# Chunked attention and gated convolution on one core: all pieces in a new order, buffers in new homes, nine first taps on VectorE

## The chip, the cores and the metric

One core of a Trainium2 chip. The core has five instruction queues: TensorE (PE in the rows, with its weight loads as PEld), VectorE (DVE), ScalarE (ACT), GpSimd (POOL) and SyncE (SP), which issues all transfers here. Each works through its own queue in order and waits on semaphores for the others. The metric is the time of one execution on the device in microseconds, lower is better.

## The reference

```python
# q, k, v: (8 batches, 8 heads, 576 tokens, 64); chunks of 64 tokens
scores = scale * np.matmul(q_c, k_c.transpose(0, 1, 2, 4, 3))   # 64 x 64 in each chunk
scores = scores - np.max(scores, axis=-1, keepdims=True)
attn = np.exp(scores)
attn = attn / (np.sum(attn, axis=-1, keepdims=True) + 1e-09)
out = np.matmul(attn, v_c)
x = np.ascontiguousarray(attn_out.transpose(0, 2, 1, 3)).reshape(B, S, H * D)   # (8, 576, 512)
for k in range(K):                                  # 5 taps along the tokens, per channel
    gate_pre += conv_w[k][None, None, :] * xp[:, k:k + S, :]
gate = 1.0 / (1.0 + np.exp(-gate_pre))
val = x @ w_val                                     # 512 x 512
return (gate * val @ w_out).astype(np.float32)      # 512 x 512
```

## The kernel before

The 8 x 576 tokens are cut into nine groups of 512 tokens. The kernel is written as short functions, called **pieces**, each one or a few instructions on one engine. A string, `ORDER`, lists some 1,130 pieces with their arguments; the loop at L599 calls them one after the other, and since `run` (L157) keeps the program order, that list is the order of every engine's queue. A second table, `SLOTS`, gives the number of the buffer that each new tile takes, in the order in which tiles are made; a tile that takes a used buffer waits until its last reader is done. So the two tables decide all waits. The time per piece, the planner that made the tables, and its model are not in the program.

For a group `g` and a half `p` of its heads, the pieces are, with their engine:

- `lq`, `lk`, `lv`: load q, k, v (SyncE, 512 KB each); `lw v c`, `lw o c`: load a quarter of the two weight matrices (512 KB); `lc`: the taps.
- `S g p b`: scores (PE, 64 x 64 tiles, into one of two PSUM buffers `big`); `mx`: row maximum (VectorE); then either `sb` (subtract, VectorE), `ex` (exp, ScalarE), `sm` (sum and reciprocal, VectorE), or `ng` (VectorE) and `ea` (sixteen exps with sums, ScalarE) and `rc` (VectorE).
- `nm`: multiply by the reciprocal (GpSimd; `nmD` on VectorE); `T`: transpose (PE into `big`); `ec`: copy out of PSUM (ScalarE; `ecD` on VectorE); `A`: attention times v (PE into `big`).
- `xc g p u`: one half of x out of PSUM (ScalarE; `xcD` VectorE); `xr`: x rounded (ScalarE); `xd`: the rest, x minus the rounded x (VectorE, reads PSUM). Instructions of two engines that touch one PSUM buffer are kept apart, reads too: `xc` placed behind an `xd` of the same buffer waits for it.
- `k0 g h`: first tap of the convolution for a quarter `h` of the channels (ScalarE; `k0D` VectorE, `k0G` GpSimd); `k g h j`: the other four taps (VectorE, 144 pieces); `sg`: tanh, which is the gate (ScalarE).
- `V g m c`: x times `w_val`, three matmuls per piece (rounded and rest of both factors), into one of four PSUM banks `ps`; `vc`: copy out (ScalarE) and `gs`: gate times value (VectorE), or `gm`, both in one straight out of PSUM (VectorE).
- `gr`: round (ScalarE); `gd`: the rest (GpSimd; `gdD` VectorE); `P g t c`: times `w_out`, three matmuls per piece, into `ps`; `oc`: copy out (ScalarE; `ocD` VectorE); `st`: store (SyncE).
- `w1` to `w7`, `wb`, `w9`: make rounded and rest parts of the weights (`w1`, `w3` and `w7` on VectorE or, with a G, GpSimd; `w4` VectorE; `w2`, `w5`, `w6` ScalarE; `wb` GpSimd, `wbD` VectorE). `F`: the first group's product with unprepared weights (PE). `W n`: n matmuls of zeros that keep PE busy. `hl`, `zr`, `zi`, `zm`, `zw`: small fills.

PE has 3,333 matmuls in all. All instructions carry the line of `run`, L158, in the rows, so tiles and shapes tell them apart: `acc` is the convolution's accumulator, `x` the attention's output, `ps` and `big` PSUM, `t`, `t2a` and the like working buffers of a pool, `v_hi`, `v_lo`, `o_hi`, `o_lo` the weights.

Of the kernel before, what the change touches and what calls it, by code (L numbers as in the profile page):

```python
# [17 lines left out]
ORDER = """zi,lk 0 0,zw,zr 1,lc,lq 0 0,lw v 2,lk 0 1,w1 c 0,S 0 0 1,w3G c 0,lq 0 1,lw v 0,mx 0 0 1,sb 0 0 1,S 0 0 0,lw v 3,  # L18
lk 1 0,W 4,ex 0 0 1,S 0 1 0,mx 0 0 0,lv 0 0,zr 0,zm,sb 0 0 0,sm 0 0 1,w5 c 0,S 0 1 1,w3G v 2,W 8,hl 0,w1G v 2,
ex 0 0 0,lq 1 0,nm 0 0 1,sm 0 0 0,T 0 0 1,w5 v 0,w2 c 0,lw v 1,w2 v 2,mx 0 1,w3 v 0,w1 v 0,lk 1 1,nm 0 0 0,w5 v 2,  # L20
mh 0 1,ec 0 0 1,T 0 0 0,ml 0 1,w4 v 2,ec 0 0 0,sp 0 1,w2 v 0,A 0 0 0,w4 c 0,ep 0 1,xc 0 0 0,lw o 0,w1 v 3,lq 1 1,
w3G v 3,lv 0 1,w7G v 2,w4 v 0,w9,A 0 0 1,w5 v 3,w5 v 1,w7 v 0,lk 2 0,S 1 0 0,w1G v 1,S 1 0 1,sm 0 1,w3 v 1,mx 1 0,
F 0 1 0,nm 0 1,lw o 3,F 0 2 0,k0 0 0,w6 v 0,xc 0 0 1,w2 v 3,sb 1 0,w2 v 1,w1G o 0,F 0 3 0,T 0 1,w4 v 3,S 1 1 0,w6 v 2,
lq 2 0,ec 0 1,S 1 1 1,ex 1 0,wb v 2,w4 v 1,wb v 0,A 0 1,lw o 2,lk 2 1,w7 v 3,w5 o 0,W 8,F 0 0 0,w7G v 1,lv 1 0,k0 0 1,
xr 0 1,F 0 2 1,mx 1 1,sm 1 0,w3G o 0,lq 2 1,sb 1 1,k 0 0 4,w1 o 3,S 2 0 0,xc 0 1 0,w2 o 0,nm 1 0,k 0 0 2,ex 1 1,
sm 1 1,xc 0 1 1,w6 v 3,S 2 0 1,xn 0 1,xe 0 1,F 0 3 1,V 0 2 2,hl 1,mx 2 0,T 1 0,sb 2 0,w6 v 1,w3 o 3,w5 o 3,w4 o 0,
F 0 1 1,nm 1 1,k 0 0 1,lq 3 0,S 2 1 0,S 2 1 1,lk 3 0,ec 1 0,lw o 1,ex 2 0,k0 0 3,A 1 0,lv 3 0,F 0 0 1,w5 o 2,mx 2 1,
w7G o 0,xc 1 0 1,wb v 3,sm 2 0,w5 o 1,sb 2 1,w1G o 2,V 0 3 2,lv 1 1,V 0 1 2,k 0 0 3,V 0 0 2,k0G 0 2,w1G o 1,xr 1 0,
w3G o 1,V 0 2 3,w6 o 0,k 0 1 1,T 1 1,xd 1 0,w2 o 2,nm 2 0,xc 1 0 0,ex 2 1,lq 4 0,V 0 0 3,V 0 3 3,ec 1 1,w2 o 3,vc 0 3,
S 3 0 0,wbD v 1,A 1 1,S 3 0 1,k 0 2 4,vc 0 2,k0 1 0,V 1 1 0,V 1 2 0,xr 1 1,sm 2 1,V 1 2 1,mx 3 0,lk 3 1,xd 1 1,  # L30
V 1 1 1,xc 1 1 0,lq 3 1,lv 3 1,ng 3 0,k 0 2 1,V 0 1 3,V 1 2 2,xc 1 1 1,sg 0 0,T 2 0,w3 o 2,lv 2 0,k 0 1 2,V 1 1 2,
gm 0 0,V 1 3 0,k 0 1 4,k 0 3 2,k 0 2 3,nm 2 1,w4 o 3,ea 3 0,k 0 3 1,V 1 2 3,k 0 1 3,k0 1 3,V 1 3 1,V 1 1 3,T 2 1,
V 1 3 2,k 0 3 4,ec 2 0,k 0 2 2,ec 2 1,S 3 1 0,k 0 3 3,vc 1 1,k0G 1 2,S 3 1 1,A 2 0,V 1 0 0,gr 0 0,w2 o 1,V 1 0 1,
rc 3 0,lk 4 0,mx 3 1,vc 1 2,k 1 0 2,hl 2,xr 2 0,V 1 0 2,sb 3 1,gd 0 0,sg 0 2,nm 3 0,xc 2 0 1,V 1 3 3,sg 0 1,W 1,
vc 1 3,xc 2 0 0,xd 2 0,k 1 2 1,gs 0 2,gm 0 1,V 1 0 3,ex 3 1,lv 2 1,w4 o 2,sm 3 1,S 4 0 0,S 4 0 1,A 2 1,vc 1 0,k0G 1 1,
k 1 0 3,V 2 0 0,xc 2 1 0,xc 2 1 1,lk 4 1,mx 4 0,k0 2 1,xr 2 1,w7 o 2,k0G 2 0,ng 4 0,k 1 0 4,V 2 1 0,sg 0 3,V 2 1 1,
wb o 0,nm 3 1,gr 0 2,V 2 0 1,k 1 1 4,lq 4 1,V 2 2 0,xn 2 1,xe 2 1,V 2 3 0,V 2 2 1,V 2 3 1,k 1 2 4,ea 4 0,T 3 0,w4 o 1,
V 2 1 2,V 2 0 2,ec 3 0,V 2 2 2,V 2 1 3,V 2 2 3,k 1 1 3,V 2 3 2,k 1 3 3,lq 5 1,vc 2 1,T 3 1,k 1 1 2,k 1 3 1,vc 2 2,
k 1 1 1,V 2 3 3,S 4 1 0,ec 3 1,vc 2 3,k 1 2 2,S 4 1 1,gr 0 1,A 3 0,k 1 3 2,k 1 0 1,sg 1 0,k 1 3 4,V 2 0 3,xr 3 0,
k 1 2 3,vc 2 0,w7 o 1,lv 4 0,gd 0 1,xc 3 0 1,P 0 2 0,w6 o 1,P 0 3 0,P 0 1 0,gd 0 2,P 0 0 0,xcD 3 0 0,xd 3 0,gs 0 3,  # L40
w6 o 2,gr 0 3,wbD o 1,A 3 1,hl 3,w7 o 3,P 0 1 1,P 0 2 1,P 0 0 1,sg 1 2,mx 4 1,ng 4 1,wbD o 2,xr 3 1,gd 0 3,k 2 0 2,
k 2 1 4,P 0 3 1,w6 o 3,wbD o 3,rc 4 0,ea 4 1,P 0 3 2,P 0 1 2,k 2 0 1,xd 3 1,xcD 3 1 1,gs 1 0,P 0 2 2,P 0 0 2,P 0 0 3,
oc 0 0,k0G 2 2,k 2 0 3,P 0 1 3,P 0 3 3,nm 4 0,lq 5 0,oc 0 1,P 0 2 3,k0 2 3,sg 1 1,T 4 0,k 2 1 2,k 2 0 4,V 3 3 0,
xc 3 1 0,k 2 2 2,oc 0 2,V 3 1 0,lk 5 0,rc 4 1,V 3 0 0,gs 1 2,lk 5 1,k 2 3 2,V 3 1 1,ec 4 0,sg 1 3,gs 1 1,S 5 0 0,
sg 2 0,S 5 1 0,k0 3 3,k 2 1 1,S 5 0 1,oc 0 3,S 5 1 1,gs 1 3,mx 5 1,gr 1 0,gd 1 0,nm 4 1,V 3 1 2,gr 1 2,V 3 1 3,
k 2 1 3,V 3 3 1,V 3 2 0,lq 6 0,mx 5 0,V 3 0 1,lk 8 0,k0 3 0,gr 1 1,k 2 2 3,sb 5 0,vc 3 1,sg 2 1,V 3 3 2,ng 5 1,
gdD 1 2,V 3 3 3,lv 4 1,gr 1 3,k 2 2 4,k0 3 2,k 2 3 1,V 3 2 1,gd 1 1,V 3 0 2,lk 6 0,vc 3 3,k 2 3 3,P 1 0 0,ea 5 1,
P 1 1 0,P 1 1 1,k 2 2 1,k 3 2 4,k 3 3 1,lq 6 1,gdD 1 3,P 1 1 2,k 2 3 4,V 3 2 2,k 3 0 2,T 4 1,V 3 0 3,k 3 2 3,k 3 0 1,
# [610 lines left out]
```

## Time and profile before

| | |
|---|---|
| median of 3 runs | 283.56 us (281.74 to 283.76) |
| the profiled execution | 281.89 us |
| its span, first to last instruction | 280.1 us |
| mean granted TensorE clock | 0.994 |
| PE busy | 258.9 us (92%) |
| VectorE busy | 239.3 us (85%) |
| ScalarE busy | 195.2 us (70%) |
| GpSimd busy | 113.1 us (40%) |
| HBM read, written | 32.53 MB, 9.44 MB |

Busy times are unions of an engine's instructions; a PE that is busy may still run its matmuls slowly. The 1.79 us between span and execution lie around the program.

### The profile page before, as it was taken

Reading aid. Unit: us, or ns where it says so; the run is one execution under the profiler, and the core shown is the slowest. Engines: PE = TensorE matmul, PEld = TensorE weight load, DVE = VectorE, ACT = ScalarE, POOL = GpSimd, SP = SyncE. Lnnn points to the kernel's source line nnn. Section 1 sums busy time; section 2 is a strip of 40 time slices with the busy share of each in tenths; the row PEclk is TensorE's granted clock in tenths of the full one; section 3 lists DMA queues with packets and bytes.
Section 4 is the critical chain, followed back from the end, with each engine's and each line's share of the span. In section 5 each row is a group of like instructions: output and inputs, shape, how many; then the busy total and the mean of one; then the engine's idle time right before and its main releaser. Section 6 shows DMA issues by size and latency. Waiting matters only on the chain.

```text
span 280.1 us, 7958 instructions
## 1 busy us (share of the span) xinstructions
PE 258.9 (92%) x3333; PEld 216.6 (77%) x3333; DVE 239.3 (85%) x330; ACT 195.2 (70%) x499; POOL 113.1 (40%) x92
## 2 busy tenths in 40 slices
...
PEclk9999999999999999999997999999999999999999
...
GB/s 230 414 412 411 400 280 53 216 92 288 77 64 239 3 94 210 150 136 170 75 118 0 307 145 192 0 120 220 6 37 0 111 5 152 0 171 16 115 187 150
DMA packets 14291, 42.47 MB, mean 152 GB/s; under 512 B 1712, under 2 KB 1712, under 8 KB 14256
## 3 DMA queue, kind: packets, MB, share of 16 engines
...
q8 instruction: 26, 0.43, 0.7%
q14 instruction: 9, 0.07, 0.1%
HBM read 32.53 MB, written 9.44 MB: 150 GB/s over the span
## 4 chain that ended last, share of the span: by engine, by line
DVE 53%; PE 21%; ACT 14%; DMA 5%; issue 5%; SPq 0%; DVEq 0%; ACTq 0%
DVE acc L158 22%; PE ps L158 19%; DVE t L158 9%; DVE mx L158 5%; DVE rs L158 5%; ACT t L158 5%; DVE e_row L158 4%; ACT e_row L158 4%; DMA acc<-in_moe_w_val 4%; ACT x L158 2%; PE big L158 2%; DMA ld<-in_q 2%; DVE t2q L158 1%; DVE x L158 1%; DVE t4a L158 1%
## 5 line engine op out<-in xcount | busy, mean ns | idle before, releaser
L158 DVE SCALAR_TENSOR_TENSOR acc<-x,cw,acc 128x516 f32<-128x516 f32 (+1 forms) x144 | 111.7, 817 | 3.2 <-ACT acc L158 2.9
L158 PE MATMUL ps<-t,v_hi 128*128 128x512 f32 x240 | 85.1, 395 | 2.9 <-ACT t2f L158 2.1
L158 PEld LDWEIGHTS ps<-t,v_hi 128*128 128x128 f32 x240 | 45.5, 190 | 11.5 <-ACT t2f L158 2.5
L158 PE MATMUL ps<-t,v_lo 128*128 128x512 f32 x120 | 45.9, 383 | 0.0
L158 POOL TENSOR_TENSOR t<-e_row,rs 128x1024 f32<-128x1024 f32 (+1 forms) x12 | 23.2, 1936 | 30.0 <-DVE rs L158 30.0
L158 PEld LDWEIGHTS big<-ld,ld 64*64 64x64 f32 x1152 | 19.5, 139 | 15.0 <-issue 9.7
L158 ACT ACTIVATE e_row<-big,mx 128x64 f32<-128x64 f32 x96 | 28.6, 357 | 2.5 <-DVE mx L158 2.5
L158 PE MATMUL big<-ld,ld 64*64 64x64 f32 x1152 | 22.0, 226 | 8.7 <-DMA ld<-in_q 6.6
L158 PE MATMUL ps<-o_hi,t 128*128 128x512 f32 x80 | 29.9, 381 | 0.0
L158 ACT COPY x<-big 128x512 f32<-128x512 f32 (+3 forms) x42 | 19.7, 520 | 12.5 <-PE big L158 6.2
L158 DVE TENSOR_REDUCE mx<-big 128x16 f32<-128x1024 f32 (+1 forms) x19 | 21.8, 1151 | 5.1 <-PE big L158 5.1
L158 PEld LDWEIGHTS ps<-t,v_lo 128*128 128x128 f32 x120 | 22.8, 190 | 3.3 <-issue 0.5
L158 ACT ACTIVATION_READ_ACCUMULATOR e_row<-big,mx 128x1 f32 x96 | 23.8, 249 | 0.0
L158 PE MATMUL big<-t,ld 64*64 64x64 f32 x1088 | 19.4, 220 | 4.4 <-issue 2.4
L158 PEld LDWEIGHTS big<-t,ld 64*64 64x64 f32 x1088 | 17.6, 135 | 6.7 <-issue 2.1
L158 ACT COPY t<-ps 128x512 f32<-128x512 f32 x27 | 16.7, 625 | 8.4 <-PE ps L158 5.8
L158 ACT ACTIVATE t<-big 128x1024 f32<-128x1024 f32 x15 | 15.8, 1077 | 7.1 <-PE big L158 7.1
L158 ACT ACTIVATE e_row<-e_row 128x1024 f32<-128x1024 f32 (+1 forms) x12 | 12.0, 1001 | 11.4 <-DVE e_row L158 11.4
L158 ACT CAST t<-big 128x1024 fp32r<-128x1024 f32 x17 | 17.3, 1019 | 2.0 <-PE big L158 2.0
L158 ACT ACTIVATE acc<-x,cw 128x516 f32<-128x516 f32 (+1 forms) x24 | 17.8, 756 | 0.0
L158 POOL TENSOR_SCALAR acc<-x,cw 128x516 f32<-128x516 f32 (+1 forms) x9 | 14.9, 1657 | 4.8 <-ACT x L158 4.8
L158 PEld LDWEIGHTS ps<-o_hi,t 128*128 128x128 f32 x80 | 15.1, 189 | 2.2
...
## 6 DMA issues: line engine op xcount, KB each, us to landing
...
```

The lines of the kernel that those rows point to most:

```text
L158: return tc.keep_in_program_order(fn(*args, **kwargs))
```

## The change

The two tables are new; no function changes. Counted by piece, first taps go from 24 on ScalarE, 3 on VectorE and 9 on GpSimd to 16, 9 and 11; the rest `gd` from 25 on GpSimd and 11 on VectorE to 18 and 18; output copies `oc` from 28 on ScalarE and 8 on VectorE to 31 and 5; `gm` from 2 to 3 (and `vc` and `gs` from 34 to 33); `xcD` from 4 to 5; one `w1` goes from VectorE to GpSimd, and one `wb` from VectorE to GpSimd. All other pieces keep their engine and number, PE's matmuls, the loads and the 21 matmuls of zeros among them. The order of loads at the start is new, and the homes of all buffers are dealt out anew.

```diff
-ORDER = """zi,lk 0 0,zw,zr 1,lc,lq 0 0,lw v 2,lk 0 1,w1 c 0,S 0 0 1,w3G c 0,lq 0 1,lw v 0,mx 0 0 1,sb 0 0 1,S 0 0 0,lw v 3,
...
+ORDER = """lq 0 0,zw,lk 0 0,lw v 0,zr 0,S 0 0 0,S 0 0 1,mx 0 0 0,zr 1,sb 0 0 0,mx 0 0 1,W 8,w1 v 0,lc,sb 0 0 1,ex 0 0 1,lw v 3,
...
-    ld="012345012350412305241203123142135013450420534024035425",
...
+    ld="012345012345012345012345123152130512341520412513202401",
...
```

VectorE's queue around `xd 2 0`, the subtraction that releases PE's `A 2 1`. Before (`t44` with `big0` is `xd 2 0`, `acc` are taps, `t2q` is `w4 o 2`, preparing a weight):

```order
L158 TENSOR_REDUCE mx1_990<-big1_906 128x16
L158 SCALAR_TENSOR_TENSOR acc1_785<-x1_541,cw_70,acc1_785 128x516
L158 TENSOR_TENSOR e_row1_65<-big1_906,mx1_990 128x16x64
L158 TENSOR_TENSOR t44_1022<-big0_943,t47_998 128x1024
L158 SCALAR_TENSOR_TENSOR acc3_880<-x1_541,cw_70,acc3_880 128x516
L158 SCALAR_TENSOR_TENSOR t2a_1025<-t22_1006,t2o_783 128x512
L158 SCALAR_TENSOR_TENSOR t28_1027<-t26_1014,ps0_347 128x512
L158 SCALAR_TENSOR_TENSOR t2q_838<-t2k_659,t2q_838 128x512
```

and after (`t4b` with `big0` is `xd 2 0`, the ISA row is `w7 o 3`, `t2i` is `w4 o 2`, `acc2<-x1` the first tap of group 1 that has come from ScalarE):

```order
L158 ISA t2f_475<-t2f_475,t2h_493 128x1024
L158 SCALAR_TENSOR_TENSOR acc0_521<-x0_151,cw_70,acc0_521 128x512
L158 SCALAR_TENSOR_TENSOR acc1_347<-x0_151,cw_70,acc1_347 128x512
L158 SCALAR_TENSOR_TENSOR acc0_521<-x0_151,cw_70,acc0_521 128x512
L158 SCALAR_TENSOR_TENSOR acc1_347<-x0_151,cw_70,acc1_347 128x512
L158 SCALAR_TENSOR_TENSOR acc0_521<-x0_151,cw_70,acc0_521 128x512 x2
L158 SCALAR_TENSOR_TENSOR t2i_654<-t2l_665,t2i_654 128x512
L158 TENSOR_REDUCE mx1_989<-big1_909 128x16
L158 TENSOR_TENSOR e_row1_65<-big1_909,mx1_989 128x16x64
L158 TENSOR_SCALAR acc2_906<-x1_668,cw_70 128x516
L158 TENSOR_TENSOR t4b_1064<-big0_943,t48_1009 128x1024
```

Two weight pieces of `w_out` and a first tap now stand ahead of the subtraction.

ScalarE's queue behind `xr 5 0`. Before (`t42` is `xr 5 0`, `x1<-big1` are the copies `xc 5 0 0` and `xc 5 0 1`, `t2n` the tanh `sg 3 3`, `t44` is `xr 5 1`, `t2f` is `oc 2 3`, the copy that empties the bank for `V 5 1 0`):

```order
L158 CAST t42_2196<-big1_2140 128x1024
L158 COPY x1_2129<-big1_2140 128x2x256
L158 ACTIVATE t2n_2214<-acc1_1571 128x192
L158 ACTIVATE t2n_2214<-acc1_1571 128x320
L158 CAST t44_2220<-big0_2094 128x1024
L158 COPY t2f_2230<-ps0_1996 128x512
L158 COPY t2i_2236<-ps1_2067 128x512
L158 COPY x1_2129<-big1_2140 128x2x64
L158 COPY x1_2129<-big1_2140 128x2x192
```

and after (`x1<-big1` 64 and 192 wide is `xc 5 0 1`, `t2k` is `vc 4 2`, `t49` is `ec 6 0`, `t2o` is `oc 2 3`, `t2q` is `oc 2 0`, the last row is `xc 5 0 0`):

```order
L158 COPY x1_2149<-big1_2082 128x2x64
L158 COPY x1_2149<-big1_2082 128x2x192
L158 COPY t2k_2237<-ps0_1980 128x512
L158 ACTIVATE t49_2240<-big0_2217 128x1024
L158 COPY t2o_2248<-ps2_2151 128x512
L158 COPY t2q_2255<-ps3_2069 128x512
L158 ACTIVATE t2e_2257<-acc2_1533 128x192
L158 ACTIVATE t2e_2257<-acc2_1533 128x320
L158 COPY x1_2149<-big1_2082 128x2x256
```

The half of the x copy that has `xd 5 0` ahead of it has moved behind the copies out of `ps`.

VectorE's queue near its end. Before, the last piece that a matmul's bank hangs on is `gs 8 1` (`t2q`), with these pieces around it:

```order
L158 SCALAR_TENSOR_TENSOR acc2_3336<-x0_3265,cw_70,acc2_3336 128x512
L158 SCALAR_TENSOR_TENSOR acc0_3305<-x0_3265,cw_70,acc0_3305 128x512
L158 TENSOR_TENSOR t2a_3521<-t2l_3443,t2k_3489 128x512
L158 SCALAR_TENSOR_TENSOR t2q_3534<-t2g_3532,t24_3487 128x512
L158 COPY t28_3570<-ps2_3467 128x512
```

and after, `gm 7 2` (`t2d<-t23,ps1`), whose bank `ps1` the matmuls of `P 6 3 0` take:

```order
L158 SCALAR_TENSOR_TENSOR acc1_3378<-x0_3203,cw_70,acc1_3378 128x512
L158 SCALAR_TENSOR_TENSOR t2d_3498<-t23_3396,ps1_3318 128x512
L158 SCALAR_TENSOR_TENSOR acc0_3315<-x0_3203,cw_70,acc0_3315 128x512
L158 SCALAR_TENSOR_TENSOR acc1_3378<-x0_3203,cw_70,acc1_3378 128x512
L158 SCALAR_TENSOR_TENSOR acc0_3315<-x0_3203,cw_70,acc0_3315 128x512
L158 SCALAR_TENSOR_TENSOR t2o_3524<-t28_3491,t27_3434 128x512
```

A value is multiplied by its gate straight out of PSUM there, with several taps still to come behind it.

## Rows read from the trace of the kernel before

**Rows 1.** Page: busy us (share) per engine; TensorE clock in 40 slices
```profile
PE 258.9 (92%) x3333; PEld 216.6 (77%) x3333; DVE 239.3 (85%) x330; ACT 195.2 (70%) x499; POOL 113.1 (40%) x92
...
PEclk9999999999999999999997999999999999999999
```

**Rows 2.** Page: the chain that ended last, by engine
```profile
DVE 53%; PE 21%; ACT 14%; DMA 5%; issue 5%; SPq 0%; DVEq 0%; ACTq 0%
```

**Rows 3.** Critical chain, its end: start us, us, what
```profile
231.91 1.22 DVE t L158
...
233.18 43.24 PE ps L158 x199
```

**Rows 4.** Stages: per engine busy us (instructions), clock, DMA, GB/s
```profile
core 0: us, PE busy (x) PEld busy (x) DVE busy (x) ACT busy (x) POOL busy (x), PEclk, DMA share, GB/s
...
7.76:66.33 58.57, 52.57 (x1026) 38.23 (x1019) 53.69 (x73) 47.75 (x105) 43.22 (x34) 1.00 0.73 284
66.33:142.50 76.17, 74.75 (x1072) 64.68 (x1073) 74.27 (x110) 63.46 (x187) 33.72 (x26) 1.00 0.38 131
142.50:152.30 9.80, 7.74 (x61) 6.18 (x63) 6.40 (x7) 5.86 (x12) 2.45 (x2) 0.83 0.11 41
152.30:233.20 80.90, 79.41 (x958) 68.81 (x949) 78.65 (x106) 59.01 (x161) 22.80 (x18) 1.00 0.30 102
```

**Rows 5.** Timeline: start us, us, engine, operation; in brackets idle before
```profile
143.15 0.59 ACT L158 COPY x<-big 128x512 f32<-128x512 f32 x1 [2.44 <-DVE t L158]
...
145.80 0.48 PE L158 MATMUL ps<-t,v_hi 128*128 128x512 f32 x1 [2.06 <-ACT t2f L158]
```

**Rows 6.** Durations: page groups (count | busy, mean ns), VectorE timelines
```profile
L158 DVE SCALAR_TENSOR_TENSOR acc<-x,cw,acc 128x516 f32<-128x516 f32 (+1 forms) x144 | 111.7, 817 | 3.2 <-ACT acc L158 2.9
...
L158 ACT ACTIVATE acc<-x,cw 128x516 f32<-128x516 f32 (+1 forms) x24 | 17.8, 756 | 0.0
...
L158 DVE TENSOR_SCALAR acc<-x,cw 128x516 f32<-128x516 f32 (+1 forms) x3 | 1.4, 478 | 0.0
...
228.57 0.68 DVE L158 COPY t2i<-ps 128x512 f32<-128x512 f32 x1
...
233.05 0.74 DVE L158 SCALAR_TENSOR_TENSOR acc<-x,cw,acc 128x516 f32<-128x516 f32 x1
...
250.95 0.69 DVE L158 TENSOR_TENSOR t2a<-t2l,t2k 128x512 fp32r<-128x512 f32 x1
```

**Rows 7.** VectorE timeline, the tail
```profile
251.55 0.69 DVE L158 SCALAR_TENSOR_TENSOR t2q<-t2g,t 128x512 f32<-128x512 f32 x1
```

**Rows 8.** Start: SyncE issues, first matmul, first VectorE reduction
```profile
1.62 0.42 SPq L158 DMA_DIRECT2D ld<-in_q  x1
...
6.57 1.98 PE L158 MATMUL big<-ld,ld 64*64 64x64 f32 x64 [6.57 <-DMA ld<-in_q]
...
7.76 0.69 DVE L158 TENSOR_REDUCE mx<-big 128x8 f32<-128x512 f32 x1 [3.28 <-PE big L158]
```

**Rows 9.** Loads: ScalarE waits that a load ended; PE
```profile
11.79 0.67 ACT L158 ACTIVATE t<-acc 128x512 uint32<-128x512 uint32 x1 [0.62 <-DMA acc<-in_moe_w_val]
...
19.08 0.68 ACT L158 ACTIVATE t<-acc 128x512 uint32<-128x512 uint32 x1 [0.52 <-DMA acc<-in_moe_w_val]
...
11.72 1.90 PE L158 MATMUL ps<-warm 128*128 128x512 bf16 x8
...
16.65 1.16 PE L158 MATMUL big<-t,ld 64*64 64x64 f32 x64 [1.29 <-ACT e_row L158]
```

**Rows 10.** Stretched VectorE instructions, and one GpSimd neighbour
```profile
13.14 0.68 DVE L158 TENSOR_SCALAR t<-acc 128x512 uint32<-128x512 uint32 x1
...
147.43 1.34 POOL L158 TENSOR_TENSOR t2s<-t,t2l 128x512 fp32r<-128x512 f32 x1 [3.83 <-ACT t2l L158]
...
147.56 1.77 DVE L158 SCALAR_TENSOR_TENSOR acc<-x,cw,acc 128x516 f32<-128x516 f32 x1
...
255.68 1.18 DVE L158 SCALAR_TENSOR_TENSOR t2c<-t2l,t 128x512 f32<-128x512 f32 x1
```

More of the change, by code (lines that the diff above doesn't have):

```diff
@@ L23 @@
[L23 to L27, printed above, removed]
@@ L43 @@
[L43 to L47, printed above, removed]
```

153 lines of the change are left out of this document (82 added, 71 removed).

## The prediction, made before the run

> **What bounds the kernel now.** I read the page's busy shares and clock slices first: PE is busy 92% of the span and VectorE 85%, at nine tenths or more of the full granted clock in all slices but one [rows 1], which looks like a TensorE-bound kernel. The chain that ended last says otherwise: 53% of it is VectorE and 21% PE [rows 2]. So I looked for the place where one hands over to the other. The end of that chain is a single unbroken run of 199 matmuls from 233.18 to 276.42 us, one last copy and the store; what released it was a VectorE subtraction (piece `xd 8 0`, 231.91 to 233.12) [rows 3]. From there to the end PE sets the time (43.24 us), and before it VectorE does.
>
> The table by stage then says what VectorE did until that handover: from its first real instruction at 7.76 to 233.18 us, that is 225.4 us, it was busy 53.69 + 74.27 + 6.40 + 78.65 = 213.0 and idle 12.4 [rows 4]. Of the idle time 4.88 us lie in 7.76 to 66.33 us, 1.90 in 66.33 to 142.50, 3.40 in the short stage 142.50 to 152.30 and 2.25 after it (each the stage's length less its DVE column, the third). What a new order can win is this idle time, the stretching of VectorE instructions by GpSimd (below), and a little at the start; what it can lose is more work on VectorE, or more PE work left behind the last handover.
>
> The stage at 142.50 has one cause that the rows show. ScalarE's copy of x waits for VectorE's `xd 5 0` until 143.15; behind it in ScalarE's queue stand a tanh, a cast and the copy `t2f` that empties a PSUM bank; PE waits 2.06 us for that copy, and after it its granted clock falls, to a mean of 0.83 of 2.4 GHz over the stage [rows 4, 5]. VectorE runs dry behind it, since the next first taps stand in the same ScalarE queue.
>
> **The change, part by part.** The order of all pieces differs, so I cost it by counting what stands ahead of the handovers, with durations from rows.
>
> *VectorE's work ahead of the last handover.* In the new order the last subtraction before group 8's matmuls is `xd 8 1`. Ahead of it stand, against `xd 8 0` before: first taps on VectorE 8 for 3 (0.478 us each), output subtractions `gdD` 10 for 6 (0.69), one more x copy (taken as 0.68), and four PSUM copies `ocD` fewer (0.68), one weight subtraction fewer (taken like `gdD`, 0.69), one clip fewer (taken like a first tap) and one tap fewer (0.74) [rows 6]. 5 x 0.478 + 4 x 0.69 + 0.68 - 4 x 0.68 - 0.69 - 0.48 - 0.74 = **+1.2 us**. What the nine first taps give back is on ScalarE, eight fewer in all at 0.76 us [rows 6]; ScalarE is busy 70% and its gain counts only where someone waits for it.
>
> *PE's work behind it.* 16 V and 51 P pieces of three matmuls stood there, now 16 V and 52 P; 43.24 us for 199 matmuls is 0.217 each [rows 3], so **+0.65 us**. This route would end 1.85 us later with all waits unchanged.
>
> *The tail.* A second handover has come closer. `P 6 3 0` now takes the PSUM bank that `gm 7 2` on VectorE frees, with 44 P pieces still to go; before, the last such VectorE piece, `gs 8 1`, ended at 252.24 [rows 7] with one copy of 0.6 us and 33 P to go, which left 252.24 + 0.6 + 33 x 0.65 = 274.3, short of 276.42. VectorE has in all 5.1 us more work now (+6 first taps 2.87, +7 `gdD` 4.83, +1 x copy 0.68, -3 `ocD` 2.04, -1 clip 0.48, -1 weight subtraction 0.69), but leaves 7.3 us more for after `gm 7 2` than it left after `gs 8 1` (7 taps, 1 `gs` at 0.69, 2 `gdD`). So `gm 7 2` comes 2.1 us earlier, at 250.1 on unchanged lateness, and 44 x 0.65 = 28.6 us of PE after it end at **278.7, 2.3 us later than before**. This route is the later of the two, and I sum by it: 281.89 + 2.3 = 284.2 us, less whatever lateness VectorE sheds ahead of it.
>
> *Start.* The first scores need q and k. Before, the small taps load stood between them and q was issued at 1.62; its landing released PE at 6.57 and PE the reduction at 7.76 [rows 8]. Now q and k are the first two issues, and an issue takes 0.42 us and a little: **-0.45**, between 0 and -0.5.
>
> *Late loads.* Weights `v 0` and `v 3` now come ahead of the second q and k, so `lv 0 0` is the eleventh big load instead of the ninth. In the trace the sixth big load ended a ScalarE wait at 11.79 and the eleventh at 19.08 [rows 9]; so `A 0 0 0`, which began at 16.65, cannot begin before about 19.1. From there 0.6 us of matmuls and 0.6 of copy put `F 0 1 0` at 20.4 against 19.13. But the warm-up matmuls that stood behind `F 0 1 0` (eight, 1.90 us [rows 9]) now stand ahead of `T 0 0 0`, in time in which PE waits anyway, so PE has 1.9 us less to do from there. I take 0; with that cover gone it costs 1.3, and at best it gains 0.6.
>
> *VectorE stretched by GpSimd.* The trace has 23 VectorE instructions that ran over 0.15 us longer than their like, 16.8 us together, each beside a GpSimd instruction; the first is at 13.14 (0.68 against 0.50) and the last at 255.68 (1.18 against 0.69). A clear one: a tap that takes 0.74 elsewhere began at 147.56, 0.13 us after a GpSimd subtraction, and took 1.77 [rows 10]. Ahead of the handover GpSimd has 39 two-input instructions instead of 43; 16.8 / 49 (all of them) = 0.34 us each, so -1.4. VectorE has nine more instructions of the kinds that read SBUF alone; 23 of about 215 such (144 taps [rows 6], 34 `gs`, subtractions and weight pieces) were hit, at 0.73 each: 9 x 23 / 215 x 0.73 = +0.7. Net **-0.6**, bounds -3 and +6 (all nine hit).
>
> The Trainium skill (SBUF — State Buffer, "Who interferes with whom") states that a VectorE instruction with two SBUF inputs contends with a GpSimd one that reads SBUF, and that whoever issues first keeps the shared port pair while the other fully blocks. By that rule the tap at 147.56 would end 0.74 us after GpSimd's at 148.77, at 149.51; it ended at 149.33, so the trace agrees. The rule speaks against moving `gd` and first taps to VectorE beside a GpSimd that is busy 40% of the span [rows 1].
>
> *Idle time of VectorE.* Up to `xd 2 0` (66.33 us) the new order gives VectorE 2.6 us more to do (one `w4` and two `w7` of the output weights, an `ecD` of 1.2 us, a first tap and an x copy, less a clip, an `rc` and a tap), with exactly the same PE work left behind it (144 P, 112 V, 18 S, 13 A, 12 T). That work lies in the 4.88 us of idle time there; I take 1.7 of it as filled, bounds 0 and 2.6. The stall at 142.50 is undone in the order: one half of that x copy now stands ahead of `xd 5 0` on ScalarE, the other well behind it, and `V 5 3 0`, the first matmul that reads `xd 5 0`, takes its bank from an older copy, `vc 4 2`, that itself waits for no VectorE instruction. Of its 3.40 us I take 2.3 as won, since a stall of that kind may come elsewhere; bounds 0 and 3.4. Together **-4.0**, between 0 and -6.
>
> **Sum.** 284.2 - 0.45 - 0.6 - 4.0 = **279.1 us** against the profiled execution's 281.89 (span 280.10 and 1.79 around it). That execution and the lowest of the three runs (281.74) agree; the median is 283.56. I put half of that distance on top: 279.1 + 0.8 = **279.9 us**. A measurement of this kernel can tell about 1% (2.8 us) from no change; the forecast, 1.0% below, lies on that line.
>
> **Rivals.** (1) The stalls only change their place. A new order built by the same rules has its own pairs of queues that block each other; 12.4 us of idle time are what such an order had. For it: all four stages have idle time [rows 4]. Against: VectorE has more to do early, and is idle less. With start and contention as above and 1 us of idle time won: 284.2 - 0.45 - 0.6 - 1 = 282.2, no change. (2) Slower: the tail. If VectorE sheds nothing, `gm 7 2` to `P 6 3 0` alone gives 284.2, and half a microsecond more of lateness ahead of it passes the 1% line (284.7): 285.2 with 1 us. Against: 2.3 us of the margin are lost only when lateness stays above 252 us, and two causes of it are gone. (3) Contention: all nine added instructions hit, +6.6 instead of +0.7: 279.1 + 5.9 = 285.0. Against: 11% of their kind were hit before. This is the skill's port rule taken at its strictest. (4) The change does nothing: PE had only 21.2 us of idle time in all [rows 1], and after 152.30 us 1.5 before the last run [rows 4]; if PE and not VectorE set the end, the new order would give what it gave. That is the same time as (1).
>
> **Chances.** Forecast 0.58 (it spreads from 277 to 281.5 on the profiled execution's level, three quarters of it below 279.1 or on the line); rivals (1) and (4) 0.24; (2) 0.11; (3) 0.07. Faster by over 1%: 0.43, the part of the forecast beyond the line; within 1%: 0.15 of the forecast and 0.24 = 0.39; slower: 0.18. Range: down to 276.3, where 3 us more idle time and contention are shed than I took; up to 285.0, the price of (2) and (3).
>
> **What would show it.** The last unbroken run of matmuls should begin behind VectorE's `gm 7 2` (a scalar_tensor_tensor that reads ps) or near it, with about 132 matmuls to go; VectorE's first reduction near 7.3; VectorE idle about 8 us between that and the handover; granted clock without the dip at 142 to 152; the sum of VectorE's busy time 4 to 5 us above 239.3 and ScalarE's about 5 below 195.2. I am wrong if PE waits long in the first 30 us for `A 0 0 0` (the loads), if VectorE's taps average more than 0.82 us, or if ScalarE's queue blocks again with VectorE idle by 10 us or more.

## The result and the profile after

The changed kernel takes **269.84 us** (median; 269.41 to 270.69) against 283.66 for the kernel before in the same comparison: ratio 0.953, 95% interval 0.948 to 0.958. It is faster, as forecast, but by 13.8 us instead of 3.7, and below the whole range (276.3 to 285.0). The profiled execution took 269.82 us (span 268.0), 12.1 us less than the profiled one of before.

The page after: busy us (share) and count per engine, the TensorE clock in 40 slices, the shares of the chain that ended last, and the group of the convolution's taps on VectorE (count | busy, mean ns | idle before):

```profile
PE 255.6 (95%) x3333; PEld 215.6 (80%) x3333; DVE 236.5 (88%) x337; ACT 192.4 (72%) x494; POOL 107.8 (40%) x89
...
PEclk9999999999999999999999999999999999999999
...
PE 81%; DVE 7%; ACT 4%; DMA 4%; issue 1%; POOL 1%; SPq 0%; DVEq 0%; ACTq 0%
...
L158 DVE SCALAR_TENSOR_TENSOR acc<-x,cw,acc 128x516 f32<-128x516 f32 (+1 forms) x144 | 108.5, 789 | 0.5
```

Beside [rows 1, 2, 6]: the chain is now 81% PE where it was 53% VectorE. No slice has a lower clock. VectorE runs seven instructions more and yet is busy 2.8 us less, and a tap takes 789 ns on average where it took 817.

The stages after (columns as in [rows 4]): about up to `A 2 1`, from there to where the last handover `xd 8 1` begins, and the rest; then the stretch from `A 2 1` to the end once more as a whole:

```profile
core 0: us, PE busy (x) PEld busy (x) DVE busy (x) ACT busy (x) POOL busy (x), PEclk, DMA share, GB/s
6.56:62.00 55.44, 52.56 (x1027) 38.09 (x1019) 54.08 (x79) 47.41 (x104) 41.62 (x33) 1.00 0.80 304
62.00:217.58 155.58, 155.14 (x2059) 135.68 (x2060) 152.08 (x216) 122.99 (x350) 59.32 (x43) 1.00 0.37 125
217.58:264.34 46.76, 46.76 (x217) 40.62 (x215) 30.05 (x44) 20.14 (x41) 6.01 (x4) 1.00 0.23 85
...
62.37:264.30 201.93, 201.86 (x2274) 176.26 (x2274) 181.76 (x258) 142.74 (x389) 65.04 (x47) 1.00 0.34 116
```

From `A 2 1` at 62.37 us to the end PE works through without a wait.

Two sums follow. **PE:** it was idle 6.00 + 1.42 + 2.06 + 1.49 = 10.97 us between the first reduction and the last handover [rows 4], and is now idle 2.88 + 0.44 = 3.32. With the first matmul 1.19 us earlier (5.38, below, for 6.57 [rows 8]) and 3.3 us less busy time for the same 3,333 matmuls, 7.65 + 1.19 + 3.3 = 12.1 us: the whole difference of the two executions. **VectorE:** its idle time over the first two stages is 1.36 + 3.50 = 4.9 us, where it was 12.4.

PE in order of time (start, us; in brackets the idle time before and its releaser). Before, `A 2 1`:

```profile
66.38 0.93 PE L158 MATMUL big<-t,ld 64*64 64x64 f32 x48 [0.64 <-DVE t L158]
```

After, the first matmul, `A 0 0 0`, `A 2 1`, and `P 6 3 0`:

```profile
5.38 1.88 PE L158 MATMUL big<-ld,ld 64*64 64x64 f32 x60 [5.38 <-DMA ld<-in_k]
...
19.02 0.69 PE L158 MATMUL big<-t,ld 64*64 64x64 f32 x32
...
62.37 0.82 PE L158 MATMUL big<-t,ld 64*64 64x64 f32 x41 [0.97 <-DMA ld<-in_v]
...
235.69 0.38 PE L158 MATMUL ps<-o_hi,t2p 128*128 128x512 f32 x1
```

VectorE, after: `xd 8 1` and `gm 7 2`, the two handovers from VectorE to PE by which the forecast summed:

```profile
217.55 1.22 DVE L158 TENSOR_TENSOR t<-big,t 128x1024 fp32r<-128x1024 f32 x1
...
234.30 0.67 DVE L158 SCALAR_TENSOR_TENSOR t2d<-t,ps 128x512 f32<-128x512 f32 x1
```

`A 2 1` has exactly the same PE work behind it in both kernels. It begins at 62.37 instead of 66.38, so 4.0 us are won ahead of it and 8.1 behind it. `gm 7 2` ends at 234.97, 0.72 us before PE comes to its bank: the handover that the forecast saw in the tail is there, but VectorE reaches it in time.

### The profile page after: what moved, and what is told of

Read it like the earlier page. It is cut to its first block, busy times and chain, and to the rows that moved or that the text cites. A ratio compares the mean times of both kernels' runs of the same rounds, so it can differ in the third digit from the quotient of the medians.

```text
span 268.0 us, 7951 instructions
## 1 busy us (share of the span) xinstructions
PE 255.6 (95%) x3333; PEld 215.6 (80%) x3333; DVE 236.5 (88%) x337; ACT 192.4 (72%) x494; POOL 107.8 (40%) x89
## 4 chain that ended last, share of the span: by engine, by line
PE 81%; DVE 7%; ACT 4%; DMA 4%; issue 1%; POOL 1%; SPq 0%; DVEq 0%; ACTq 0%
PE ps L158 65%; PE big L158 16%; ACT e_row L158 3%; DVE mx L158 2%; DMA ld<-in_v 2%; DVE rs L158 2%; DMA ld<-in_k 2%; DVE e_row L158 1%; POOL t L158 1%; DVE acc L158 1%; ACT t L158 1%; DVE t4a L158 0%; SPq L158 0%; DVE t2d L158 0%; ACT t2h L158 0%
## 5 line engine op out<-in xcount | busy, mean ns | idle before, releaser
L158 DVE SCALAR_TENSOR_TENSOR acc<-x,cw,acc 128x516 f32<-128x516 f32 (+1 forms) x144 | 108.5, 789 | 0.5
L158 PE MATMUL ps<-t,v_hi 128*128 128x512 f32 x208 | 74.0, 389 | 0.0
L158 PEld LDWEIGHTS ps<-t,v_hi 128*128 128x128 f32 x208 | 39.3, 189 | 6.1 <-issue 0.2
L158 PE MATMUL ps<-o_hi,t 128*128 128x512 f32 x108 | 39.9, 383 | 0.0
L158 POOL TENSOR_TENSOR t<-e_row,rs 128x1024 f32<-128x1024 f32 (+1 forms) x16 | 30.3, 1896 | 15.9 <-DVE rs L158 11.6
L158 ACT ACTIVATE e_row<-big,mx 128x64 f32<-128x64 f32 x96 | 28.6, 368 | 0.7 <-DVE mx L158 0.7
L158 ACT COPY t<-ps 128x512 f32<-128x512 f32 x22 | 13.1, 594 | 20.2 <-PE ps L158 20.0
L158 POOL TENSOR_SCALAR acc<-x,cw 128x516 f32<-128x516 f32 (+1 forms) x11 | 21.7, 1973 | 7.4 <-ACT x L158 4.5
L158 PEld LDWEIGHTS ps<-o_hi,t 128*128 128x128 f32 x108 | 20.4, 189 | 3.0
L158 POOL COPY x<-x 128x16 f32<-128x16 f32 x8 | 4.2, 529 | 38.5 <-DVE acc L158 38.5
L158 PE MATMUL big<-ident,t 128*128 128x128 f32 x136 | 17.7, 273 | 0.6 <-DVE e_row L158 0.5
```

The costliest lines, as they stand in the source:

```text
L158: return tc.keep_in_program_order(fn(*args, **kwargs))
```

## Experiments

Each run is set against runs of the kernel before on the same chip (281.3 to 286.3 us; the ratio with its 95% interval). In the texts of what was expected, theory A is the first one formed after the result: VectorE set the pace before, TensorE sets it after.

| run | us | ratio |
|---|---|---|
| e1 before, stall undone | 279.84 | 0.989 (0.986 to 0.992) |
| e2, e10 before, taps' load later | 282.60, 282.12 | 0.998 (0.995 to 1.001), 0.993 (0.990 to 0.997) |
| e3 after, six first taps back | 270.08 | 0.955 (0.952 to 0.958) |
| e4 after, eleven subtractions back | 274.60 | 0.970 (0.966 to 0.974) |
| e5, e7 before, more PE, more VectorE | 285.34, 286.61 | 1.009 (1.006 to 1.013), 1.013 (1.008 to 1.017) |
| e6, e8 after, more PE, more VectorE | 272.43, 273.50 | 0.964 (0.961 to 0.968), 0.968 (0.964 to 0.972) |
| e9, e15 before, subtractions off GpSimd | 284.64, 284.86 | 1.005 (1.002 to 1.008), 1.005 (1.002 to 1.009) |
| e11, e12 after, `lv 2 1` early; and halves | 269.07, 269.94 | 0.949 (0.947 to 0.950), 0.952 (0.950 to 0.954) |
| e13 new head, old rest | 275.64 | 0.975 (0.971 to 0.979) |
| e14 old head, new rest | 279.84 | 0.989 (0.986 to 0.991) |
| e16 as e13, stall undone | 273.44 | 0.966 (0.963 to 0.969) |
| e17 before, seven zero matmuls out | 282.81 | 0.997 (0.994 to 1.000) |
| e18 after, again | 269.77 | 0.951 (0.948 to 0.954) |

### e1: the stall at 142 us alone

```diff
-V 4 1 1,xd 5 0,xc 5 0 0,V 4 1 2,
+V 4 1 1,xd 5 0,V 4 1 2,
...
-oc 2 3,V 5 1 0,oc 2 1,V 4 1 3,
+oc 2 3,V 5 1 0,oc 2 1,xc 5 0 0,V 4 1 3,
```

> The kernel before, with one piece moved: the x copy `xc 5 0 0` on ScalarE goes behind `oc 2 1`, so that the copies that free PSUM banks no longer stand behind VectorE's `xd 5 0`. Theory A (the change gains because VectorE idles and is stretched less, in many places, of which the stage at 142 us is one): VectorE's 3.4 us idle time there fall away and reach the end through the last handover, 280 to 281 us against 283.7, granted clock 1.0 in the stage. Rival R1 (stalls only change place): the stage is clean but VectorE idles elsewhere by as much, 283 to 284. Rival R2 (the lost clock and the stall are the bulk of the gain): 277 or less.

The same stretch of time as the third row of [rows 4], in e1:

```profile
142.50:152.30 9.80, 9.80 (x169) 8.57 (x168) 9.77 (x12) 8.08 (x16) 4.56 (x3) 1.00 0.23 82
```

PE and VectorE are busy throughout, the clock is whole, and 1.1% (3.1 us) come off the time. That is nearly all of VectorE's 3.40 us of idle time there. Theory A's number holds (279.84, just under its 280 to 281); R1 (stalls only change place) and R2 (the bulk of the gain) fall.

### e2 and e10: the earlier start alone

```diff
-zi,lk 0 0,zw,zr 1,lc,lq 0 0,lw v 2,lk 0 1,w1 c 0,S 0 0 1,w3G c 0,lq 0 1,
+zi,lk 0 0,zw,zr 1,lq 0 0,lw v 2,lk 0 1,S 0 0 1,lc,w3G c 0,lq 0 1,
...
-sb 0 0 1,S 0 0 0,
+sb 0 0 1,w1 c 0,S 0 0 0,
```

That is e2. In e10 `lc` stands behind `lk 0 1`, `w1 c 0` behind `sb 0 0 0`, and `w3G c 0` behind `w3G v 2`.

> The kernel before, with the small load of the taps issued behind the first q and k halves instead of between them (its first use, `w1 c 0` on VectorE, behind the first subtraction). Theory A: first matmul 0.45 to 1.2 us earlier than 6.57, and the time lower by that and no more, 282.5 to 283.2 against 283.7. Rival R3 (what is gained at the start is lost by the first wait on a later load): first matmul earlier, time unchanged, 283.7.

> The kernel before, with the load of the taps behind the first loads of q and k as in the run e2, but its first uses on VectorE and GpSimd behind more of the first scores' work, so that VectorE's queue does not wait for the late load. Theory D (the earlier first matmul reaches the end once nothing waits for the late load): first matmul near 5.5 instead of 6.6 to 7.9, and 1 to 2 us off the time, 281 to 282 against 282.8. Rival R3 (the head is bound by the later loads or by VectorE's work): under 0.5 us.

e2 gains nothing that can be told. Its first matmul begins at 5.54 us:

```profile
5.54 1.98 PE L158 MATMUL big<-ld,ld 64*64 64x64 f32 x64 [5.54 <-DMA ld<-in_q]
```

Its VectorE begins its reduction a microsecond earlier and then stands in the queue for the late taps:

```profile
6.73 0.69 DVE L158 TENSOR_REDUCE mx<-big 128x8 f32<-128x512 f32 x1 [5.62 <-PE big L158]
...
9.52 0.18 DVE L158 TENSOR_SCALAR cw_t<-raw_cw 128x20 f32<-128x20 f32 x1 [1.37 <-DMA raw_cw<-in_moe_conv_w]
```

With that wait out of the way, e10 gains 0.7% (1.9 us; the interval is 1.0 to 2.8). So the times bear theory D out for the kernel before, and the start is worth about three to four times the 0.45 us forecast. A part of the 1.9 us may be the clock: 4 of the 8 executions of e10 that are compared have a mean clock of 0.994 or less, and 16 of the 19 of before. The executions above that average 281.3 us in e10 and 282.6 before, a gain of 1.3. No trace shows where the gain arises, since the one of e10 is of one of its longest executions (284.79 us).

### e3: the first taps on VectorE, undone

```diff
-k0D 2 1,
+k0 2 1,
...
```

The same for 2 3, 4 0, 7 1, 7 2 and 8 2.

> The changed kernel, with six of its nine first taps on VectorE put back on ScalarE, where they were before (groups and quarters 2 1, 2 3, 4 0, 7 1, 7 2, 8 2), at the same places of the order. Theory A (the order carries the gain and PE sets the end from 62 us on): VectorE 2.9 us less busy, ScalarE 4.6 us more, time within 1 us of 269.8. Rival R4 (the taps on VectorE carry it, since ScalarE's late first taps made VectorE idle): VectorE waits for ScalarE's taps again by 3 us or more, 273 or more.

270.08 against 269.8: no change. The part that the change is named after carries none of the gain (R4 falls). But VectorE was to be 2.9 us less busy, and it is not:

```profile
PE 255.3 (95%) x3333; PEld 215.5 (80%) x3333; DVE 236.4 (88%) x331; ACT 195.3 (73%) x500; POOL 108.8 (41%) x89
```

Six instructions fewer and the same busy time: counted as the prediction counted (VectorE instructions over 0.15 us longer than their like), the stretching is about 12 us where the changed kernel has about 10, though no instruction of GpSimd was moved.

### e4: eleven subtractions back on GpSimd

```diff
-gdD 0 2,
+gd 0 2,
...
```

The same for 0 3, 2 2, 3 0, 3 3, 4 3, 5 2, 6 0, 6 1, 6 3 and 7 1.

> The changed kernel, with eleven of its output subtractions put back from VectorE to GpSimd, where they were before, at the same places of the order. Theory A: VectorE has 7.6 us less to do, more of its instructions run beside GpSimd's and stretch (from 9.9 us towards 14), and PE still sets the end, within 1.5 us of 269.8. Rival R5 (less GpSimd beside VectorE carries the gain): stretching back to 17 us or more and the time up by 3 us or more, 273 or above, because the rounded rests then come late for PE.

4.8 us more. The page's engine line says where it starts:

```profile
PE 257.5 (94%) x3333; PEld 216.4 (79%) x3333; DVE 241.0 (88%) x326; ACT 192.5 (70%) x494; POOL 124.4 (46%) x100
```

VectorE has eleven instructions less and is busy 4.5 us more than in the changed kernel; the eleven took at least 0.60 us each, so the instructions that are left stretch by over 11 us more (counted one by one, 30 instructions by about 21 us, where the changed kernel has 17 by about 10). And the handover of the forecast appears, `gm 7 2` and then `P 6 3 0`:

```profile
238.22 0.68 DVE L158 SCALAR_TENSOR_TENSOR t2d<-t,ps 128x512 f32<-128x512 f32 x1
...
238.95 0.80 PE L158 MATMUL ps<-o_hi,t2p 128*128 128x512 f32 x1 [2.24 <-DVE t2d L158]
```

The windows around it, with the clock in the third column from the right:

```profile
236.20:238.95 2.75, 0.51 (x3) 0.11 (x1) 2.75 (x4) 1.12 (x3) 0.89 (x1) 0.99 0.00 0
238.95:242.65 3.70, 3.70 (x9) 3.01 (x10) 3.67 (x6) 1.23 (x2) 1.03 (x1) 0.54 0.00 0
```

After 2.24 us of idle PE the granted clock is 0.54 of 2.4 GHz over 3.7 us, near its lower level of 1.2, so the wait is paid nearly twice. Theory A's "within 1.5 us" was wrong, R5's time and its stretching right.

### e5 to e8: whose work is on the path

PE: the first matmul of each of group 3's output tiles three times more (2.6 us). VectorE: group 4's `gs` twice (2.4 us). Each in both kernels.

```diff
+        for _ in range(3 if g == 3 and c == 0 else 0):
+            run(E.matmul, o_ps[g, t], lhsT=gh[g, c][:, ts], rhs=in_turn(wh["o"][:, c, :]), start=True, stop=True)
```

```diff
-        run(on.scalar_tensor_tensor, out=gt[g, m], in0=gate[g, m], scalar=1.0, in1=v_sb[g, m], op0=ALU.add, op1=ALU.mult)
+        for _ in range(2 if g == 4 else 1):
+            run(on.scalar_tensor_tensor, out=gt[g, m], in0=gate[g, m], scalar=1.0, in1=v_sb[g, m], op0=ALU.add, op1=ALU.mult)
```

> The kernel before, with 12 more matmuls: the first matmul of each output tile of group 3 is done three times more (it overwrites, so the result stays). 12 x 0.217 = 2.6 us of TensorE work between 158 and 171 us, where VectorE and not TensorE should set the pace. Theory A (VectorE sets the end before the change): 0 to 0.8 us more, up to 283.9. Rival R6 (TensorE sets it already before): 2.6 us more, 285.7.

> The changed kernel with the same 12 more matmuls in group 3's output. Theory A (TensorE sets the end from 62 us on after the change): the whole 2.6 us are paid, 272.2 to 272.8 against 269.8. Rival R7 (after the change VectorE still sets the end, only earlier): under 1 us more, below 270.8.

> The kernel before, with group 4's four multiplications of gate and value on VectorE done twice (the same output again). Back to back they begin 0.60 us apart, so 4 x 0.60 = 2.4 us of VectorE work near 182 us. Theory A (VectorE sets the end before the change): 2 to 2.6 us more, 285.2 to 285.8 against 283.1. Rival R6 (TensorE sets it already before): under 0.8 us more.

> The changed kernel with the same doubled multiplications of group 4 on VectorE, 2.4 us. Theory A (VectorE has slack after the change): 0 to 0.7 us more, below 270.6. Rival R7 (VectorE still sets the end): 2.4 us more, 272.2.

| added | before | after |
|---|---|---|
| 2.6 us of PE | +2.6 us (1.6 to 3.7) | +2.6 us (medians) |
| 2.4 us of VectorE | +3.6 us (2.3 to 4.8) | +3.7 us (medians) |

e6 went as theory A says, and e7 in its direction, with 3.6 us for its 2 to 2.6; the other two went against it. PE's work was already on the path before (R6 for PE), and VectorE has no slack after, at the places where the work was put. The traces show how. VectorE's subtraction `xd 6 1` waits for ScalarE's copies of that x, which stand behind copies of PE's output; in e5 that wait grows by 2.5 us. Before, and then in e5:

```profile
177.61 1.23 DVE L158 TENSOR_TENSOR t<-big,t 128x1024 fp32r<-128x1024 f32 x1 [1.97 <-ACT x L158]
```

```profile
180.91 1.23 DVE L158 TENSOR_TENSOR t<-big,t 128x1024 fp32r<-128x1024 f32 x1 [4.45 <-ACT x L158]
```

In e7 PE's wait for VectorE ahead of the transpose `T 7 1` is 2.65 us, where it was 0.69, and the clock behind it falls:

```profile
195.14 0.30 PE L158 MATMUL big<-ident,t4a 128*128 128x128 f32 x1 [2.65 <-DVE e_row L158]
```

```profile
195.14:200.00 4.86, 4.86 (x19) 4.29 (x20) 4.86 (x8) 3.06 (x6) 2.33 (x3) 0.65 0.09 33
```

In e8 PE, which has no wait behind `A 2 1` in the changed kernel, has four, 2.8 us together; the longest is for group 4's `gdD 4 3`:

```profile
185.88 0.48 PE L158 MATMUL ps<-o_hi,t2q 128*128 128x512 f32 x1 [1.16 <-DVE t2q L158]
```

So neither engine could take on this work for nothing in either kernel. The view that one sets the pace and the other has room, on which the forecast was built, is too simple: before the change each waits for the other in turn. In e8 the 2.4 us also shift VectorE against GpSimd, and the page shows 4.8 us more busy time than after, not 2.4 (stretched instructions: 19 by about 12 us, against 17 by about 10):

```profile
PE 256.7 (94%) x3333; PEld 215.2 (79%) x3333; DVE 241.3 (89%) x341; ACT 192.0 (71%) x494; POOL 109.1 (40%) x89
```

### e9 and e15: the kernel before with subtractions off GpSimd

```diff
-gd 3 0,
...
-k 4 3 3,
+k 4 3 3,gdD 3 0,
...
```

In e15 likewise `gdD 1 1` behind `k 2 2 3`, `gdD 2 1` behind `k 3 0 4`, `gdD 4 3` behind `k 6 1 1`, `gdD 5 3` behind `gr 5 3` and `gdD 5 2` behind `k 7 2 4`; e9 has `gdD 6 3` and `gdD 6 1` behind `xd 8 0` and `gdD 7 1` behind `gs 7 2` too.

> The kernel before, with nine of its 25 GpSimd output subtractions done on VectorE instead, each placed right behind the VectorE instruction that it had stretched (or behind its own input). Six of them stand ahead of the last handover `xd 8 0`: they cost VectorE 6 x 0.60 to 0.69 = 3.6 to 4.1 us of its own work. Theory C (a subtraction on GpSimd that hits VectorE costs it about 1 us, more than doing it costs): the stretching that these hit instructions showed, 0.52 + 0.71 + 1.03 + 1.03 + 1.02 + 0.57 + 1.02 = 5.9 us ahead of the handover, goes, and the time falls by 1.5 to 2.5 us, 280.5 to 281.5 against 282.8. Rival R8 (moving it costs VectorE its own time, and others are hit in place of these): 2 to 4 us more, 285 to 287.

> The kernel before, with six of its GpSimd output subtractions on VectorE (1 1, 2 1, 3 0, 4 3, 5 2, 5 3), all ahead of the last handover, each placed behind the VectorE instruction that it had stretched or behind its own input. Their own work is 3.6 to 4.1 us, the stretching that they caused 5.9 us. Theory C (a subtraction that hits costs more on GpSimd than on VectorE): 1.0 to 2.5 us off, 281.1 to 282.6 against 283.6. Rival R8 (others are hit in their place): no change or up to 4 us more.

Both are 0.5% slower. e9, which moves three more behind the handover, was ill built: behind `xd 8 0` VectorE waits 2.22 us for PE, and PE in turn 1.41 us. e15 has no such place, and its VectorE is busy 240.9 us, 1.6 more than before, for 4 us of added work: some 2.5 us of stretching went. But the stall at 142 us became longer: PE waits 2.59 us in it instead of 2.06, and VectorE 3.28 instead of 2.9. VectorE in e15 there, the next tap waiting for its first tap on ScalarE:

```profile
152.34 0.68 DVE L158 TENSOR_TENSOR t2s<-t,t2l 128x512 fp32r<-128x512 f32 x1
156.31 0.76 DVE L158 SCALAR_TENSOR_TENSOR acc<-x,cw,acc 128x516 f32<-128x516 f32 x1 [3.28 <-ACT acc L158]
```

So in the old order the move does not pay (theory C falls as a gain, and R8 is right in sign), though in the new order its undoing costs 4.8 us (e4). What a subtraction costs on GpSimd hangs on where it falls.

### e11 and e12: more of the head

```diff
-A 2 0,vc 1 1,lk 5 0,w4 o 2,
+A 2 0,vc 1 1,lv 2 1,w4 o 2,
...
-k0 1 1,lv 2 1,xc 2 0 0,
+k0 1 1,lk 5 0,xc 2 0 0,
```

Their buffers change places too. e12 has this and, at the very start, `lq 0 0 0,lk 0 0 0,lq 0 0 1,lk 0 0 1` for `lq 0 0,lk 0 0`.

> The changed kernel, with the load `lv 2 1`, for which TensorE waits 0.97 us at 62.37 us, issued ahead of `lk 5 0`, which is needed 33 us later (the two change places and buffers). Theory A (TensorE sets the end from 62 us on): 0.7 to 1.0 us less, 268.8 to 269.2 against 269.8. Rival R7 (VectorE, which trails the same place, takes the gain away): under 0.3 us.

> As e11, and the first loads of q and k are split into halves (q, k, q, k), so that the first scores need 256 KB of each instead of 512 KB. Theory D (the start reaches the end): the first matmul 0.5 to 1.2 us earlier than 5.4, and the time 0.5 to 1.2 us below e11's, 267.7 to 268.6. Rival R3 (the later loads are delayed by two more issues and the head gives it back): as e11 or up to 0.5 us above it.

`A 2 1` in e11, and the first matmul and `A 2 1` in e12:

```profile
61.42 0.76 PE L158 MATMUL big<-t,ld 64*64 64x64 f32 x40
```

```profile
4.26 1.03 PE L158 MATMUL big<-ld,ld 64*64 64x64 f32 x28 [4.26 <-DMA ld<-in_k]
...
62.00 0.70 PE L158 MATMUL big<-t,ld 64*64 64x64 f32 x36
```

e11's `A 2 1` begins 0.95 us earlier, and its times are 0.7 to 0.8 us below the changed kernel's (269.00 to 269.16, against 269.41 to 270.69 and 269.57 to 270.12 in its two timings), as theory A expected. By the mark set for e18 below, this is not shown: e11's ratio lies inside e18's interval (0.948 to 0.954), not under it. The times themselves do not overlap, but they come from different comparisons. e12's first matmul is 1.1 us earlier than the changed kernel's, yet `A 2 1` comes 0.6 later than e11's and the time is 0.9 us above e11's. So theory D falls for the split, and R3 is right, and more: the head gives it all back.

> The changed kernel again, unchanged, for a narrower interval: ratio 0.953 +- 0.002 to the kernel before. If e11's earlier load is worth the 0.77 us that its first timing showed, e11's ratio (0.9489, 0.9474 to 0.9504) lies below this one's whole interval; if not, the two overlap in their middles.

### e13, e14, e16: the two heads exchanged

e13 is the changed kernel's list up to and with `A 2 1`, then what is still to be done in the old list's order and on its engines; e14 the other way round. e16 is e13 with e1's edit. The pieces that the old list had done by then and the new one not follow right behind the cut, in e13:

```diff
 A 2 1,
+lv 3 1,rc 3 0,k 1 0 2,nm 3 0,sg 0 1,vc 1 3,k 1 2 1,gs 0 1,gm 0 2,sm 3 1,
```

> The changed kernel's order, engines and buffers up to and with `A 2 1`, and behind it all that is left in the order and on the engines of the kernel before (the buffers of that rest dealt out anew, always the one free for longest). Theory E (the head carries what the stage at 142 us, the start and the subtractions leave): A 2 1 near 62.4 us instead of 66.4 to 69.2, and 4 to 6 us off the time, 277.6 to 279.6 against 283.6. Rival R9 (an earlier head is eaten by the waits behind it): under 2.5 us off, 281 or more.

> The other way round: order, engines and buffers of the kernel before up to and with `A 2 1`, then what is left in the order and on the engines of the changed kernel. Theory E: A 2 1 near 66.4 to 69.2, and 4 to 6 us above 269.8, 273.8 to 275.8. Rival R9 (the rest of the new order has room for a late head): under 2.5 us above, 272.3 or less.

> e13 with the copy `xc 5 0 0` moved as in e1. If head and stall are separate terms, e13's gain and e1's 3.2 us add up: 274.4 to 276.4. If the new head had already cleared the stall (VectorE comes earlier to `xd 5 0`), the time is that of e13.

The head alone is worth **2.5% (7.1 us)**, more than theory E's 4 to 6; the new rest alone 1.2% (3.3 us), so that e14 lies 10.1 us above the changed kernel, where theory E had 4 to 6; together they gave 4.7% (13.3). The first 55 us in e13 and then in e14, same columns:

```profile
7.00:62.00 55.00, 52.31 (x1015) 37.81 (x1007) 53.65 (x79) 47.23 (x103) 42.01 (x34) 1.00 0.80 302
```

```profile
7.00:62.00 55.00, 48.15 (x919) 34.94 (x923) 50.06 (x68) 41.23 (x94) 37.05 (x30) 1.00 0.74 281
```

Every engine does more in the same time in the new head: PE 4.2 us, VectorE 3.6 us and 11 instructions. `A 2 1` begins at 62.34 in e13 and 68.46 in e14, whose first matmul came at 7.49:

```profile
7.49 0.81 PE L158 MATMUL big<-ld,ld 64*64 64x64 f32 x20 [7.49 <-DMA ld<-in_q]
...
68.46 0.75 PE L158 MATMUL big<-t,ld 64*64 64x64 f32 x36 [0.62 <-DVE t L158]
```

From the first matmul to `A 2 1` the old head takes 59.8 us in the profile of before and 60.3 to 61.1 in six other profiles with it and the old loads; the new head takes 56.6 to 57.0 in eight profiles. So 3 to 4 us are won in the head besides the start.

e16 takes 2.2 us more off e13, so stall and head are separate terms. The stall's is smaller than the 3.1 us of e1, and e13's trace shows a reason. PE's wait is still there, but the clock behind it stays whole, so that only the wait is left to win:

```profile
141.14 0.48 PE L158 MATMUL ps<-t,v_hi 128*128 128x512 f32 x1 [1.96 <-ACT t2p L158]
```

```profile
141.14:146.00 4.86, 4.86 (x59) 4.13 (x63) 3.61 (x4) 3.24 (x7) 1.35 (x1) 1.00 0.01 2
```

The two halves' gains do not add up to the whole; 3 us need both. Counted in the profiled executions from `A 2 1` to the end of the span, the old rest takes 213.7 us behind the old head and 211.5 behind the new one, the new rest 209.6 and 205.6. So each rest is shorter behind the new head. For the old rest the clock that stays whole can be most of it; the new rest's 4.0 us are not tested (in e14 PE waits 1.62 us inside `A 2 1` and 0.44 us later, in the changed kernel it does not).

### e17: zero matmuls in the old head

```diff
-w5 o 0,W 8,F 0 0 0,
+w5 o 0,W 1,F 0 0 0,
```

> The kernel before, with one matmul of zeros instead of eight between `A 0 1` and `F 0 0 0` (25.4 to 27.3 us in its trace). Theory F (TensorE's queue is the bound there): the seven, 7 x 0.237 = 1.7 us, come off the head and 1 to 1.7 us off the time, 282 to 282.7 against 283.7. Rival R10 (VectorE and the waits for it set the old head): TensorE idles instead, under 0.5 us either way.

0.3% less, not to be told from none: R10 is the nearer, but up to 1.7 us is not excluded.

## Why the prediction was wrong

**Right.** The stall at 142 us was read rightly, its cause and that the new order undoes it. The late loads, taken as 0, did not hold up the head: `A 0 0 0` begins at 19.02, where "not before about 19.1" was said, and `A 2 1` all the same 4.0 us earlier than before. No run prices them alone, and a later load, `lv 2 1`, still makes PE wait 0.97 us (e11). The tail was read rightly as a mechanism: 44 P pieces at 0.65 us behind `P 6 3 0` give 235.69 + 28.6 = 264.3, where PE ended, and in e4 the wait appears at just this place.

**Wrong: the lateness that VectorE sheds ahead of `gm 7 2`.** That instruction was to end at 250.1 us on unchanged lateness, less 0.45 + 0.6 + 4.0 = 5.05 us. That is 245.0. It ended at 234.97, 15.1 earlier than on unchanged lateness. All three terms were too small:

- *Start*, -0.45 (0 to -0.5): -1.19 in the profiled execution. The issue moved by 0.46 us as said; but from the last needed issue to the first matmul it now takes 5.38 - 1.16 = 4.22 us, where it took 6.57 - 1.62 = 4.95 [rows 8]. In e2, where only the taps' load moves from between the two loads, it takes 5.54 - 1.16 = 4.38. So what is issued between them changes how fast the first ones land, and only the issue had been counted. In six other profiles with the old loads the first matmul came at 7.5 to 8.2 us, so the execution of [rows 8] had an early start. e10 puts the term at 1.9 us, or 1.3 at a like clock.
- *Idle time of VectorE*, -4.0 (0 to -6): 12.4 to 4.9 us up to the last handover, -7.5. In the head it was bounded at 2.6 us, the work that was added there, as if idle time went only where other work fills it. It also goes where what VectorE waits for comes earlier: 4.88 us became 1.36. For the stall 2.3 of 3.40 us were taken, with a part kept back for new stalls; e1 got 3.1.
- *Contention*, net -0.6 (-3 to +6; its two parts, -1.4 and +0.7, make -0.7): VectorE was to be 4 to 5 us busier (5.1 by the sum of the work) and is busy 2.8 less. Counted as the prediction counted, the stretching fell from 16.8 us to about 10 over the whole run, and by about 6.4 up to the last handover. The estimate put a mean number of hits on each kind of instruction, and 0.34 us on each two-input instruction of GpSimd. In the new order eleven subtractions cost over 11 us (e4), in the old one six cost some 2.5 (e15). Nor does a change of GpSimd's work have to come in: e3 and e8 leave it as it is and shift VectorE alone, and each has about 2 us more stretching. A count of instructions cannot give that, and the trace of before could not show it for an order that had not run.

Together the three make 1.2 + 7.5 + 6.4 = 15.1 us. That this agrees to the tenth is luck, since added work and the stretch behind the handover are not in it.

**Wrong: one engine as the bound.** The chain of waits [rows 2, 3] gave VectorE the time up to the last handover, and PE's 5 us of waits after 66 us were priced at nothing. e5 shows 2.6 us of PE work fully paid in the kernel before. Hence rival (4), "if PE sets the end, the new order gives what it gave", was built on a false choice: PE gained its own 7.65 us of waits and 3.3 us of busy time. Of the latter the lowered clock behind the stall is about 1.7 us by an estimate (6.5 us at a mean of 0.74, from the row in the last section); the rest was not traced.

**Wrong: the head as one stage of four.** It got 2.15 us (1.7 and 0.45) of the forecast and carries 7.1 us alone (e13), with what the whole clock gives back in e13 included. What is left of that after the start's 1.9 (e10) is not split further: e17 does not find it in the zero matmuls.

**Wrong: half the distance to the median, +0.8.** The median of before lies above its profiled execution, and the early start of that execution is a likely part of the reason; after, the two agree (269.84 and 269.82). If so, the change removes the distance, and it should not have gone on top. No run shows this alone. Also, 279.9 is 1.3% below the median of 283.56; the prediction's "1.0%" holds only for 279.1 against 281.89, so that by its own numbers the forecast lay beyond the line and not on it.

**Named marks.** The clock dip at 142 to 152 us is gone, as said. Taps average 0.789, under the mark of 0.82. VectorE's first reduction begins at 6.56, not near 7.3, and its idle time is 4.9, not 8. ScalarE is busy 2.8 us less, not 5. The last unbroken run of PE begins not behind `gm 7 2` with 132 matmuls to go but at `A 2 1`, 62.37 us, with 2,274. None of the "I am wrong if" cases came; all of them looked for a loss.

What stays open: why VectorE is stretched less in the new order (e3 and e8 show that timing alone moves the stretching by about 2 us, but no run tests the whole 7), where in the head its 3 to 4 us arise, and the 3 us that head and rest give only together.
